# Moving the points of sums, products and score visits in a three-engine schedule of attention and a gated MLP

## Chip, cores, metric

The kernel runs on one core of one Trainium2 chip. The metric is the device time of one execution in microseconds (us). The traces record it at full or at half speed. Engines: PE is TensorE, DVE is VectorE, ACT is ScalarE, POOL is GpSimd, SP issues DMA transposes.

## The reference

Eight batches of gated attention with squared ReLU scores, then an MLP with g = h cos(h):

```python
B, S, D = u.shape                      # 8, 3008, 256; z has 64 columns
scores = np.matmul(z, z.transpose(0, 2, 1)) / S
attn = np.maximum(scores, 0.0) ** 2
x = (u * np.matmul(attn, v)).reshape(B * S, D)
h = x @ w_in                           # 256 -> 2048
out = (h * np.cos(h)) @ w_out          # 2048 -> 256
```

## The kernel before

Each batch has six column groups c of 512 tokens. The scores are symmetric, so a block (c, R) with R > c is computed once (a "score visit" computes up to three half blocks) and a DMA transpose makes its mirror (R, c).

```python
def s_squares(b, c, R, p, banks, on_act=False):      # cut
    ... nc.scalar.activation(rt[:, i, :], banks[i], AF.Relu)          # ACT
    ... nc.vector.tensor_tensor(sq, rv, rv, ALU.mult)                 # DVE (or ACT)
    if p == 1 and R > c ...: turn_s(b, c, R)                          # SP: DMA transpose
```

In 44 of the 48 groups (all but the first four of batch 0) attn @ v isn't multiplied out plainly over row blocks 0 to 4. As in Strassen's method, seven products replace eight: DVE first forms sums of quarters of the score blocks in place. `a_sums1` is the first, `a_sums2` the second, and products P1 to P7 read raw quarters (P1, P2, P4), first sums (P5, P6) and second sums (P3, P7):

```python
def a_sums1(b, c, team):                                 # cut
    s1 = quarters(b, c, team, (0, 1))                    # overwritten in place
    nc.vector.tensor_tensor(s1, s1, quarters(b, c, team, (1, 1)), ALU.add)         # L486
    nc.vector.tensor_tensor(s2(b, c, team[0], len(team)), s1,
                            quarters(b, c, team, (0, 0)), ALU.subtract)            # L488
def a_sums2(b, c, R):
    nc.vector.tensor_tensor(dst, src, sub, ALU.subtract)                           # L498
def keep(b, c, n):                                       # cut: combines the products
    if n in (1, 5): nc.scalar.copy(p15[:, n // 5, 0:h], acc[n // 5][:, h:2 * h])   # L544
    elif n == 6:    nc.vector.tensor_tensor(q[:, 0, 0:h], acc[0][:, h:2 * h],
                                            p15[:, 1, 0:h], ALU.add)               # L546
    elif n == 8:    ...   # RADD, L549        else: ...   # WADD, L555
def finish(b, c):                                        # cut: x = acc * u, frees acc
    nc.vector.tensor_tensor(x[:, nh, :], acc[nh][:, o:o + n], ut[:, nh, o:o + n], ALU.mult)  # L415
```

P1, P4, P6 and P7 go one after the other into the same columns of one PSUM bank (PSUM is the memory that PE's results go to), so the addition after P6 (L546) must have read them before P7 may write. Beside this run the MLP's matmuls (`h_quantum` L564 on PE, cos on ACT, g on DVE L571; `y_quantum` L581 on PE), which fill PE between the pieces.

Everything is put on a clock of 48 units per batch, 8 per group; the list of events is sorted by time, and that is the program order:

```python
at(t + SUM1[c][0] + 2 * SUM1[c][1] * i, 2, lambda: a_sums1(b, c, team))
at(t + SUM2[c][0] + SUM2[c][1] * i, 2.5, lambda: a_sums2(b, c, R))
at(t + o, 2, lambda: product(b, c, n))              # o from PLAN[c]; "A1"/"B1": a plain block
at(t + o + 0.02, 2.1, lambda: keep(b, c, n))        # after products 1, 5, 6, 7
at(t + 7.45, 2, lambda: finish(b, c))
t = b * span - lead + span * (i + VSHIFT.get(i, 0)) / len(visits)
scores.append((2 * math.floor(t / 2) + 1.2, some))  # score visit i
```

Of the kernel before, what the change touches and what calls it, by code (L numbers as in the profile page):

```python
# [14 lines left out]
def kernel(  # L15
# [32 lines left out]
    NSLOT = 18  # L48
    NW = 5
    PLAN = {  # L50
        0: [(0.75, 'P1 P2'), (1.0, 'P5'), (1.4, 'P6'), (2.75, 'P3'), (3.0, 'P7'),
            (5.0, 'P4'), (5.4, 'A1'), (6.15, 'A1'), (6.35, 'A1'), (6.55, 'B1'),
            (7.0, 'B2')],
        1: [(0.75, 'P1 P5 P2'), (2.15, 'P6'), (2.75, 'P7 P3'), (3.4, 'A2 B1'),
            (4.35, 'P4 B1'), (6.75, 'A1 B1')],
        2: [(0.75, 'P1 P5 P2'), (2.15, 'B1'), (2.35, 'P6'), (2.75, 'P7 B1'), (3.4, 'P3'),
            (4.15, 'P4'), (6.55, 'A1'), (6.75, 'A1'), (7.4, 'A1 B1')],
        3: [(0.75, 'P1 P2'), (1.0, 'P5'), (1.4, 'P6'), (2.75, 'P7'), (3.0, 'B1'),
            (3.4, 'P3'), (4.35, 'A1 B1'), (4.75, 'A1'), (5.4, 'B1'), (6.15, 'P4'),
            (6.75, 'A1')],  # L60
        4: [(0.75, 'P1 P2'), (1.0, 'P5'), (1.4, 'P6'), (4.15, 'P7'), (4.75, 'B1'),
            (5.4, 'P3 B1'), (6.35, 'P4 A1'), (7.0, 'A1'), (7.4, 'A1 B1')],
        5: [(0.75, 'P1 P2'), (1.4, 'P5'), (2.75, 'P6'), (3.0, 'P3'), (4.15, 'B1'),
            (4.55, 'P7'), (5.0, 'P4'), (5.4, 'B1'), (6.15, 'A1'), (6.55, 'A1'),
            (7.4, 'A1 B1')],
    }
    SUM1, SUM2, WADD, RADD = {0: (-3.5, 0.07), 1: (-2.25, 0.5), 2: (-1.85, 0.15), 3: (-2.85, 0.85), 4: (-3.05, 0.85), 5: (-2.3, 0.55)}, {0: (1.1, 0.02), 1: (0.8, 0.32), 2: (2.1, 0.02), 3: (1.45, 0.02), 4: (1.1, 0.17), 5: (1.55, 0.02)}, {0: 4.36, 1: 3.06, 2: 4.96, 3: 4.16, 4: 6.06, 5: 5.76}, {0: 2.05, 1: 3.35, 2: 3.55, 3: 5.25, 4: 4.25, 5: 0.95}
    TSUM = [-1.9, 0.5, -0.4]
    WSET = {0: [0, 1, 2, 3, 4], 1: [0, 1, 2, 3, 4], 2: [0, 1, 2, 3, 4], 3: [0, 1, 2, 3, 4], 4: [0, 1, 2, 3, 4], 5: [0, 1, 2, 3, 4]}
    VAT = [-13, -3.9, -4.5]  # L70
    HOFF, YOFF = [0.3, 0.3, 0.4, 0.6], [0.6, 0.6, 0.6, 0.7]
    HALF = {0: 3.3, 1: 4.75, 2: 6.9, 3: 6.0, 4: 9.2, 5: 4.7}

    inv_s = 1.0 / float(S)
    inv_s2 = inv_s * inv_s
# [156 lines left out]
    def direct(b, c, R):  # L232


        return b == 0 and c <= 2

    def triangle(b, c, R):

        return R == c and (b, c) > (0, NC // 2)
# [190 lines left out]
    def v_sums(b, g):  # L430

        n = min(2, NW - 2 * g)
        t = vs(b, g)[:, 0:n * K, :].rearrange("p (r k) (d w) -> p r k d w", r=n, w=P)
        o = vsum[:, 2 * g:2 * g + n]
        for d in range(2):
            ins = nc.vector.tensor_tensor(
                o[:, :, 2 * d], t[:, :, 2 * d:2 * d + 2, 1], t[:, :, 0:2, d], ALU.subtract).ins
            if d == 0:
                after(ins, before[-1], NOSYNC)
        nc.vector.tensor_tensor(o[:, :, 1], t[:, :, 2:4, 1], o[:, :, 0], ALU.subtract)  # L440
        nc.vector.tensor_tensor(o[:, :, 3], t[:, :, 2:4, 0], o[:, :, 1], ALU.subtract)
        for R in range(2 * g, 2 * g + n):
            summed[R] = b
# [156 lines left out]
    def at(t, rank, f):  # L600
        events.append((t, rank, len(events), f))
# [4 lines left out]
    groups = [(c, R) for c in range(NC) for R in range(c, NC)]  # L606
    span = NC * U
    lead = 2.0 * U
    VSHIFT = {4: 0.0, 13: 0.55, 1: 0.54, 5: 0.0, 2: 0.0, 12: 1.09, 10: 0.27, 7: 0.55, 0: 0.28, 6: 0.29, 9: -0.82, 3: -0.28, 11: 0.54, 8: 0.0}

    items = [(c, R, p) for c, R in groups for p in ((2,) if c == R else (0, 1))]
    for c, before_item in {5: (4, 5, 0)}.items():
# [8 lines left out]
    visits = []  # L621
# [10 lines left out]
    for b in range(B):  # L632
        for i, some in enumerate(visits):
            some = [(b, c, R, q) for c, R, p in some if not direct(b, c, R)
                    for q in ((0, 1) if p == 2 and not triangle(b, c, R) else (p,))]
            t = b * span - lead + span * (i + VSHIFT.get(i, 0)) / len(visits)
            if some:
                scores.append((2 * math.floor(t / 2) + 1.2, some))
        for c in range(NC):
            if direct(b, c, c):  # L640
                for i in range(NC):
                    R = (c + i) % NC
                    scores.append((c * U + 4 * i / 3 - 3.1, [(b, c, R, 0), (b, c, R, 1)]))
# [19 lines left out]
    for t, some in scores:  # L663
        for b, c, R, p in some:
            use(("a", b, c, R), t, t + 1)
            if p == 1 and R > c and TURNS.get((b, c, R), t) is not None:
                t = TURNS.get((b, c, R), t)
                use(("t", b, c, R), t + 0.8, t + 2.5)
                use(("a", b, c, R), t, t + 3)
    for b in range(B):  # L670
        for g in range((NW + 1) // 2):
            at(b * span + (TSUM[g] if b else 3 * U + 1 + 2.5 * g), 2, lambda b=b, g=g: v_sums(b, g))
        for c in range(NC):
            t = b * span + c * U
            W = seven(b, c)
            d = direct(b, c, c)
            ready = 1.5 + when[(b, c, NC - 1)]
            first, last = (0.6, 6.93) if d else (HALF[c] if W else 1.0, 7.3)
            room = [i for i, sc in enumerate(scores)
# [60 lines left out]
    for m in range(NT):  # L740
        b, i = divmod((m + 1) * TW - 1, S)
# [10 lines left out]
    for b in range(B):  # L752
        t = b * span
# [73 lines left out]
```

## Time and profile before

| | before |
|---|---|
| time, 3 runs | 1226.01 us median, 1224.46 to 1227.6 |
| profiled span | 1222.9 us |
| busy PE, DVE, ACT | 1199.4, 1060.5, 864.1 us |
| PE idle in the span | 23.5 us |
| DMA transposes of score blocks | 249 |

One more stretch of the order of time is needed later, a score visit (visit 9) of the kernel before; columns are start, us, engine, line, what, and the idle time before it:

```profile
330.12 0.84 PE L261 MATMUL w<-zT 64*128 64x512 f16 x4
331.19 0.39 PE L261 MATMUL w<-zT 64*128 64x512 f16 x2 [0.23 <-DVE g L571]
331.41 0.39 PE L365 MATMUL acc<-s,v 64*128 64x512 f16 x2
```

The visit begins at 330.12 and the next matmul (L564) at 331.73, so it took 1.61 us. Only 0.23 us of that is recorded as idle.

### The profile page before, as it was taken

The page shows a single profiled execution, that of the slowest core. Times are in us where ns is not written, and L with a number is a line of the kernel's source. Part 1 is how long each engine was busy: PE and PEld are TensorE (multiplying, and loading weights), DVE is VectorE, ACT ScalarE, POOL GpSimd, SP SyncE. Part 2 cuts the span into 40 slices and gives each one's busy share as a digit, 9 for nine tenths or more (in the row PEclk, how much of TensorE's full clock was granted, in tenths as well). Part 3 has the DMA queues.
Part 4 walks back from the last instruction along what each step waited for, and adds up shares of the span by engine and source line. Part 5 has one row for each costly group of instructions (what it writes and reads, how often), then busy time and mean ns, then how long its engine had stood idle before and what let it go on. Part 6 is the DMA issues. An engine that isn't in the chain of part 4 may idle for free.

```text
span 1222.9 us, 23870 instructions
## 1 busy us (share of the span) xinstructions
PE 1199.4 (98%) x8853; PEld 808.8 (66%) x8853; DVE 1060.5 (87%) x1977; ACT 864.1 (71%) x1783; POOL 145.9 (12%) x201
## 2 busy tenths in 40 slices
PE   8999999999999999999999999999999999999998
PEld 3356766667667666676666766676666676666776
DVE  7889988899889898898988989889898899888974
ACT  6768686686866868668686687766877668776645
POOL 3220101001010110101101010011100111000000
PEclk9999999999999999999999999999999999999999
DMA  9999857789578986769778698776996769764411
GB/s 149 180 162 156 126 99 111 124 146 119 105 110 122 150 111 119 101 119 150 113 121 106 110 156 113 124 107 99 166 112 123 98 102 169 119 111 85 73 35 44
DMA packets 484228, 145.07 MB, mean 119 GB/s; under 512 B 432400, under 2 KB 484112, under 8 KB 484112
## 3 DMA queue, kind: packets, MB, share of 16 engines
q1 hardware_dynamic: 356448, 88.73, 42.7%
q0 software_dynamic: 100400, 29.77, 26.8%
q10 hardware_dynamic: 27264, 25.06, 6.8%
q8 instruction: 69, 1.13, 0.4%
q14 instruction: 47, 0.39, 0.1%
HBM read 60.29 MB, written 24.64 MB: 69 GB/s over the span
## 4 chain that ended last, share of the span: by engine, by line
PE 85%; DMA 7%; ACT 3%; DVE 3%; issue 1%; POOL 0%; DVEq 0%; ACTq 0%; POOLq 0%
PE acc L530 26%; PE w L564 23%; PE w L581 23%; PE acc L388 6%; DMA s<-s 6%; PE w L261 6%; ACT rt L317 2%; DVE g L571 2%; PE acc L365 1%; DMA w_out<-in_moe_w_out_dram 1%; ACT s L321 1%; DVE x L415 1%; ACT c L568 0%; DVE s L323 0%; PE w L784 0%
## 5 line engine op out<-in xcount | busy, mean ns | idle before, releaser
L568 ACT ACTIVATE c<-w 128x512 f16<-128x512 f32 x752 | 413.2, 628 | 138.6 <-PE w L564 62.5
L571 DVE TENSOR_TENSOR g<-w,c 128x512 f16<-128x512 f32 x752 | 475.9, 681 | 36.0 <-ACT c L568 34.0
L564 PE MATMUL w<-x,w_in 128*128 128x512 f16 x1504 | 368.6, 379 | 1.0 <-ACT rt L317 1.0
L581 PE MATMUL w<-w_out,g 128*128 128x256 f16 x3008 | 358.5, 273 | 1.6 <-DMA w_out<-in_moe_w_out_dram 1.6
L581 PEld LDWEIGHTS <-g 128*128 128x128 f16 x3008 | 294.2, 98 | 76.0 <-issue 4.3
L317 ACT ACTIVATE rt<-w 128x512 f16<-128x512 f32 x489 | 251.5, 612 | 38.2 <-PE w L261 38.2
L564 PEld LDWEIGHTS <-w_in 128*128 128x128 f16 x1504 | 145.7, 98 | 158.5 <-issue 13.9
L530 PE MATMUL acc<-s,vsum 128*128 128x256 f16 (+1 forms) x1760 | 216.1, 270 | 1.8 <-DVE s L486 1.8
L530 PEld LDWEIGHTS <-vsum 128*128 128x128 f16 x1760 | 169.3, 98 | 37.5 <-issue 13.4
L323 DVE TENSOR_TENSOR s<-rt 128x1024 f16<-128x1024 f16 x196 | 132.3, 687 | 56.5 <-ACT rt L317 55.8
L530 PE MATMUL acc<-s,v 128*128 128x256 f16 (+1 forms) x1320 | 157.7, 270 | 9.2 <-DVE x L415 9.2
L118 POOL DMA_DIRECT2D ust<-in_u_dram x112 | 81.0, 730 | 616.3 <-PE acc L388 402.0
L530 PEld LDWEIGHTS <-v 128*128 128x128 f16 x1320 | 127.4, 98 | 27.1 <-issue 12.3
L588 ACT ACTIVATE ob<-w 128x256 f32<-128x256 f32 x188 | 76.1, 405 | 85.3 <-PE w L581 85.1
L498 DVE TENSOR_TENSOR s<-s,s 128x1024 f16<-128x1024 f16 (+1 forms) x220 | 136.1, 669 | 0.0
L388 PE MATMUL acc<-s,v 128*128 128x512 f16 x448 | 133.4, 382 | 0.4 <-DVE s L323 0.3
L261 PE MATMUL w<-zT 64*128 64x512 f16 (+3 forms) x684 | 93.8, 360 | 4.1 <-DVE g L571 1.9
L486 DVE TENSOR_TENSOR s<-s 128x1024 f16<-128x1024 f16 (+2 forms) x132 | 76.4, 583 | 19.9 <-DMA s<-s 19.5
L488 DVE TENSOR_TENSOR s<-s 128x1024 f16<-128x1024 f16 (+2 forms) x132 | 76.5, 584 | 1.1
L388 PEld LDWEIGHTS <-v 128*128 128x128 f16 x448 | 39.4, 98 | 50.3 <-issue 25.0
L544 ACT COPY p<-acc 128x256 f32<-128x256 f32 (+1 forms) x88 | 32.7, 372 | 55.4 <-PE acc L530 54.7
L415 DVE TENSOR_TENSOR x<-acc,ut 128x512 f16<-128x512 f32 (+7 forms) x112 | 64.3, 595 | 1.5 <-PE acc L388 1.5
(39 smaller groups left out, 440.6 us busy)
## 6 DMA issues: line engine op xcount, KB each, us to landing
out_dram<-ob ACTq DMA_DIRECT2D x92, 256.0 KB, 2.8
ust<-in_u_dram POOLq DMA_DIRECT2D x80, 128.0 KB, 5.0
v<-in_v_dram POOLq DMA_DIRECT2D x16, 512.0 KB, 7.6
s<-s SPq DMA_TRANSPOSE x249, 4.4
v<-in_v_dram POOLq DMA_DIRECT2D x8, 448.0 KB, 5.9
zst<-in_z_dram POOLq DMA_DIRECT2D x14, 128.0 KB, 4.9
ust<-in_u_dram POOLq DMA_DIRECT2D x16, 96.0 KB, 3.8
w_in<-in_moe_w_in_dram POOLq DMA_DIRECT2D x4, 256.0 KB, 5.8
```

The costliest lines, as they stand in the source:

```text
L118: hold(nc.gpsimd.dma_start(dst, src))
L261: chain(nc.tensor.matmul(out, zt[h, R * K + k + 1 - lo, :], zt[h, j0 + s0:j0 + K, :].rearrange("p j w -> p (j w)"), start=True, stop=True, ...
L317: nc.scalar.activation(rt[:, i, :], banks[i], AF.Relu)
L323: ins = nc.vector.tensor_tensor(sq, rv, rv, ALU.mult).ins
L388: chain(nc.tensor.matmul(acc[:, 0:wn], vs(b, j // G)[:, j % G, nh * P:(nh + 1) * P], a, start=(start and n == 0), stop=(last and n == len( ...
L415: ins = nc.vector.tensor_tensor(x[:, nh, :], acc[nh][:, o:o + n], ut[:, nh, o:o + n], ALU.mult).ins
L498: after(nc.vector.tensor_tensor(dst, src, sub, ALU.subtract).ins, before[-1], NOSYNC)
L530: chain(nc.tensor.matmul(acc[bank][:, cols], lhs[:, k, :], rhs[:, k, :] if old else rhs[:, :, k * P:(k + 1) * P], start=(n in (1, 5) and i ...
L564: chain(nc.tensor.matmul(hp, w_in16[:, k, ft * P:(ft + 1) * P], x[:, k, :], start=(k == 0), stop=(k == NDH - 1)))
L568: nc.scalar.activation(c16, hp, AF.Sin, bias=math.pi / 2.0, scale=inv_s2)
L571: nc.vector.tensor_tensor(gs[(m, ft // FG)][:, ft % FG, :], hp, c16, ALU.mult)
L581: chain(nc.tensor.matmul(ys[m][:, 0:D], gs[(m, f4)][:, ft % FG, ts * P:(ts + 1) * P], w_out16[:, ft, :], start=(ft == 0), stop=(ft == NFT ...
```

## The change

Its intent is to put the sums further behind the DMA transposes that still read the blocks they overwrite, and to move the products and visits to match. Work, operands and counts stay the same. VFIRST equals VSHIFT, so it does nothing by itself. The diff, unchanged context cut:

```diff
--- before.py
+++ after.py
@@ -48,28 +48,25 @@
-        0: [(0.75, 'P1 P2'), (1.0, 'P5'), (1.4, 'P6'), (2.75, 'P3'), (3.0, 'P7'),
-            (5.0, 'P4'), (5.4, 'A1'), (6.15, 'A1'), (6.35, 'A1'), (6.55, 'B1'),
-            (7.0, 'B2')],
-        1: [(0.75, 'P1 P5 P2'), (2.15, 'P6'), (2.75, 'P7 P3'), (3.4, 'A2 B1'),
-            (4.35, 'P4 B1'), (6.75, 'A1 B1')],
-        2: [(0.75, 'P1 P5 P2'), (2.15, 'B1'), (2.35, 'P6'), (2.75, 'P7 B1'), (3.4, 'P3'),
-            (4.15, 'P4'), (6.55, 'A1'), (6.75, 'A1'), (7.4, 'A1 B1')],
-        3: [(0.75, 'P1 P2'), (1.0, 'P5'), (1.4, 'P6'), (2.75, 'P7'), (3.0, 'B1'),
-            (3.4, 'P3'), (4.35, 'A1 B1'), (4.75, 'A1'), (5.4, 'B1'), (6.15, 'P4'),
-            (6.75, 'A1')],
-        4: [(0.75, 'P1 P2'), (1.0, 'P5'), (1.4, 'P6'), (4.15, 'P7'), (4.75, 'B1'),
-            (5.4, 'P3 B1'), (6.35, 'P4 A1'), (7.0, 'A1'), (7.4, 'A1 B1')],
-        5: [(0.75, 'P1 P2'), (1.4, 'P5'), (2.75, 'P6'), (3.0, 'P3'), (4.15, 'B1'),
-            (4.55, 'P7'), (5.0, 'P4'), (5.4, 'B1'), (6.15, 'A1'), (6.55, 'A1'),
-            (7.4, 'A1 B1')],
+        0: [(0.75, 'P1 P2'), (1.0, 'P5'), (1.4, 'P6'), (2.75, 'P7'), (4.15, 'P3'),
+            (5.0, 'P4'), (5.4, 'A2 B1'), (6.55, 'A1'), (6.75, 'B2')],
+        1: [(0.75, 'P1 P2'), (1.0, 'P5'), (2.15, 'P6'), (3.0, 'P7 P3'), (3.4, 'P4 A1'),
+            (6.15, 'A1'), (6.35, 'A1 B1'), (6.55, 'B1'), (7.4, 'B1')],
+        2: [(0.75, 'P1'), (1.0, 'P5 P2'), (1.4, 'P6'), (2.75, 'P7'), (3.0, 'P3 B1'),
+            (3.4, 'B1'), (4.15, 'P4'), (6.15, 'A1'), (6.35, 'B1'), (6.55, 'A2')],
+        3: [(1.0, 'P1 P2'), (1.4, 'P5'), (2.15, 'P6'), (2.75, 'P7'), (3.0, 'P3'),
+            (3.4, 'A1'), (4.15, 'P4 B2'), (5.0, 'A2 B1')],
+        4: [(0.75, 'P1 P2'), (1.0, 'P5'), (1.4, 'P6'), (2.75, 'P7'), (4.75, 'B1'),
+            (5.4, 'P3 B1'), (6.55, 'A1'), (6.75, 'P4 A1'), (7.4, 'A1 B1')],
+        5: [(0.75, 'P1 P2'), (1.4, 'P5'), (2.75, 'B1'), (3.0, 'P3'), (4.15, 'P6'),
+            (4.55, 'P7'), (5.0, 'P4'), (5.4, 'B1'), (6.15, 'A1'), (7.4, 'A2 B1')],
-    SUM1, SUM2, WADD, RADD = {0: (-3.5, 0.07), 1: (-2.25, 0.5), 2: (-1.85, 0.15), 3: (-2.85, 0.85), 4: (-3.05, 0.85), 5: (-2.3, 0.55)}, {0: (1.1, 0.02), 1: (0.8, 0.32), 2: (2.1, 0.02), 3: (1.45, 0.02), 4: (1.1, 0.17), 5: (1.55, 0.02)}, {0: 4.36, 1: 3.06, 2: 4.96, 3: 4.16, 4: 6.06, 5: 5.76}, {0: 2.05, 1: 3.35, 2: 3.55, 3: 5.25, 4: 4.25, 5: 0.95}
-    TSUM = [-1.9, 0.5, -0.4]
+    SUM1, SUM2, WADD, RADD = {0: (-3.5, 0.07), 1: (-2.5, 0.7), 2: (-0.6, 0.15), 3: (-1.85, 0.6), 4: (-2.55, 0.85), 5: (-2.3, 0.55)}, {0: (1.1, 0.12), 1: (1.05, 0.22), 2: (2.1, 0.02), 3: (1.45, 0.12), 4: (1.1, 0.22), 5: (1.55, 0.02)}, {0: 4.86, 1: 3.56, 2: 4.36, 3: 3.56, 4: 6.76, 5: 6.26}, {0: 4.05, 1: 4.35, 2: 2.85, 3: 5.25, 4: 5.15, 5: 2.95}
+    TSUM = [-1.4, 0.5, -1.9]
-    HOFF, YOFF = [0.3, 0.3, 0.4, 0.6], [0.6, 0.6, 0.6, 0.7]
-    HALF = {0: 3.3, 1: 4.75, 2: 6.9, 3: 6.0, 4: 9.2, 5: 4.7}
+    HOFF, YOFF = [0.3, 0.3, 0.3, 0.6], [0.6, 0.6, 0.6, 0.7]
+    HALF = {0: 4.8, 1: 3.15, 2: 4.0, 3: 8.4, 4: 9.2, 5: 4.7}
@@ -606,7 +603,8 @@
-    VSHIFT = {4: 0.0, 13: 0.55, 1: 0.54, 5: 0.0, 2: 0.0, 12: 1.09, 10: 0.27, 7: 0.55, 0: 0.28, 6: 0.29, 9: -0.82, 3: -0.28, 11: 0.54, 8: 0.0}
+    VSHIFT = {4: -0.01, 13: 0.82, 1: 0.82, 5: -0.27, 2: -0.29, 12: 0.54, 10: 0.0, 7: 1.09, 0: 0.28, 6: 0.02, 9: -0.28, 3: -0.28, 11: -0.01, 8: -0.82}
+    VFIRST = VSHIFT
@@ -633,7 +631,7 @@
-            t = b * span - lead + span * (i + VSHIFT.get(i, 0)) / len(visits)
+            t = b * span - lead + span * (i + (VSHIFT if b else VFIRST).get(i, 0)) / len(visits)
```

## The prediction

> **What bounds the kernel now.** I read the busy shares first, then the waits of TensorE (PE), then the order of time around the largest of them, then the windows by batch. The page's first part:
>
> ```profile
> PE 1199.4 (98%) x8853; PEld 808.8 (66%) x8853; DVE 1060.5 (87%) x1977; ACT 864.1 (71%) x1783; POOL 145.9 (12%) x201
> ```
>
> PE is the bound, and it is idle for only 1222.9 - 1199.4 = 23.5 us of the whole span. Busy is not yet "at its peak", so I checked the pace: in the order of time a stretch of eight 512-column matmuls takes 1.90 us (shown below), and with 0.38 us for the last one that is (1.90 - 0.38)/7 = 0.217 us from start to start. Nothing in the change alters the number, shape or operands of a matmul. So what the change can win lies in PE's gaps. The view of waits of PE, first for the span after 80 us, then two of its lines for the whole span:
>
> ```profile
> PE acc L530 <- DVE x L415: 9.2, 7, 2.0
> PE w L261 <- DVE g L571: 1.9, 8, 0.3
> PE acc L530 <- DVE s L486: 1.8, 3, 0.9
> ...
> PE w L581 <- DMA w_out<-in_moe_w_out_dram: 1.6, 1, 1.6
> PE w L261 <- ACT zT L224: 1.6, 2, 1.1
> ```
>
> (us in total, times, longest.) After the first 80 us three kinds of wait are left, 9.2 + 1.9 + 1.8 = 12.9 us. Everything else is the start (first turns of z, w_out) and the tail, which the change doesn't touch. The seven waits of 9.2 us come once per batch, 152 us apart. One of them, in order of time (start, us, engine, line, what, and in brackets the idle time before it):
>
> ```profile
> 331.73 1.90 PE L564 MATMUL w<-x,w_in 128*128 128x512 f16 x8
> ...
> 337.37 1.91 PE L581 MATMUL w<-w_out,g 128*128 128x256 f16 x16
> ...
> 339.61 0.69 DVE L486 TENSOR_TENSOR s<-s 128x1024 f16<-128x1024 f16 x1 [2.19 <-DMA s<-s]
> 340.22 0.68 DVE L415 TENSOR_TENSOR x<-acc,ut 128x512 f16<-128x512 f32 x1
> 340.82 0.68 DVE L488 TENSOR_TENSOR s<-s 128x1024 f16<-128x1024 f16 x1
> 340.96 1.25 PE L530 MATMUL acc<-s,v 128*128 128x256 f16 x10 [1.67 <-DVE x L415]
> ```
>
> The reader is to see a chain. A sum of group 2 (L486) overwrites in place a block of squared scores that a DMA transpose still reads. It waits 2.19 us for it. Behind it in VectorE's (DVE's) queue stands L415, the multiplication by u that empties group 1's accumulator, and PE's first product of group 2 (L530) needs that accumulator. So the DMA is charged to PE although the product itself didn't need it. Group 3 has the milder form: its last sum waits for a DMA and product 5 reads that sum directly (the 1.8 us). VectorE's view of waits gives the source in one line:
>
> ```profile
> DVE s L486 <- DMA s<-s: 19.5, 14, 2.6
> ```
>
> Fourteen waits, 19.5 us, of which PE feels 9.2 + 1.8 = 11.0; the rest falls in VectorE's slack. A window of one batch, 188:340 us, shows how much slack:
>
> ```profile
> 188.00:340.00 152.00, 149.79 (x1128) 103.40 (x1128) 134.45 (x253) 109.89 (x229) 17.87 (x24) 1.00 0.78 121
> ```
>
> (PE, weight load, DVE, ACT, POOL busy, clock, DMA share, GB/s.) VectorE has 152 - 134.45 = 17.6 us free per batch, 12%, so shifting its order is possible, but not by much at one place.
>
> **What the Trainium skill says.** "Perfetto Trace Analysis", the section Per-instruction lifecycle, says that ACT and DVE take their instructions strictly first in, first out, and that waiting for semaphores lies outside the recorded window. The fence above agrees: L415's inputs were complete (group 1's last matmuls end by 335.8), it still started at 340.22, behind the blocked L486, and the block shows as an idle gap of 2.19 us. The same section says that a DMA's recorded issue doesn't hold the data movement. Agreed too: here the transpose in question was issued at 332.43, its record is 2 us long, but it landed at 339.52, 7.1 us later. The view of tile s gives 2.3/4.4/12.5 us from issue to landing for all transposes (shortest, median, longest). "DMA: Bandwidth & Descriptors", section Issuing engines are not separate DMA queues, says that transfers of all issuers interleave on the same engines; this fits 7.1 us where the median is 4.4, as two loads of u were issued at 332.10, though no run here isolates it.
>
> **The change part by part.** Nothing is added or removed; VFIRST equals VSHIFT. The program's clock has 48 units per batch, so a unit is 152/48 = 3.17 us. For each group I worked out from the numbers in the diff how far a sum stands behind the score visit that starts the transpose it depends on (units, before -> after): group 1's last pair 2.55 -> 3.1; group 2's last pair 1.55 -> 2.8; group 3's last block 1.35 -> 3.35; group 4's last block 3.15 -> 5.65; groups 0 and 5 stay at 3.6 and more. The two shortest, 1.55 (4.9 us) and 1.35 (4.3 us), are those where the waits are. From the visit's place to landing is some 9 us in the case above (visit on PE at about 330, landed 339.52), and the new distances are 2.8 x 3.17 = 8.9 us and 10.6 us, to which VectorE's own lag behind PE of 1.5 to 2 us is added. So both waits for the DMA should go.
>
> Group 2, step by step. The sums move from -1.85 to -0.6 with 0.3 per team: now 15.4, 15.7, 16.0, with the emptying of group 1 at 15.45. So only the first team (1.37 us: L486 and L488 at 0.68 each) stands in front of L415, and it has no young transpose. L415 then ends in time or nearly so: VectorE's g products end near 337.3 (they hang on ACT), plus 1.37, plus 0.68 for the first half makes 339.3, where PE arrives at 339.2. That removes 9.2 us. But product 5 now follows the sums closely. PE from the point 16.0 (335.6) to product 5's fourth block: eight h matmuls 1.73, sixteen y matmuls 1.75, product 1 1.09 and three blocks 0.65 = 5.2 us, so 340.9. VectorE: 337.3 + 1.37 + L415 1.36 + second team 0.83 + L486 0.68 = 341.5. A new wait of about 0.6 us, which may be 0 if the scheduler sends L486s ahead, so I take 0.4 x 7 batches = 2.8 us. Net gain 6.4 us.
>
> Group 3: its visit 11 comes 2 units earlier, the sum stays at 24.55. Gain 1.8 us. Its second team now stands right before the emptying of group 2 (23.35 against 23.45): 1.37 + 1.3 us on VectorE in the 3.5 us that PE spends on h and y before product 1. No wait expected.
>
> Visits 7 and 8 trade places, so the two-pair visit instead of the three-pair one stands before visit 9, where PE waits 0.24 us in each batch for a PSUM buffer (the 1.9 us). I take half: 1.0 us.
>
> The many moved P, A and B points (PLAN) mostly fall in stretches with no other PE event between old and new place (24.75 to 25.0, 34.75 to 36.15), so PE's order hardly changes; L365's half blocks stay next to a visit, so no more switches between 64 and 128 rows. I count 0. Sum: 6.4 + 1.8 + 1.0 = 9.2 us, 1226.0 - 9.2 = 1216.8 us.
>
> **The rivals.** (1) The wait only moves: L486 now holds up product 5 of group 2 instead of L415 holding up product 1. Against it, 1.25 units more distance for the DMA; for it, the 0.6 us of working above. If the DMA is still late the full 1.3 us a batch comes back, and the time is 1223. (2) VectorE or ACT becomes the bound where visits bunch: 10 and 11 now follow each other at 19.2 and 21.2. For it, VectorE's 88% in the batch; against it, visits 12, 13 and 0 are spread out (27.2, 31.2, 33.2 instead of 29.2, 31.2, 33.2), and today three visits in a row cost only 0.24 us. It would add 0.3 to 0.6 us a batch, 1219 to 1221. (3) All waits go, and with them the slower restart after each: 1226 - 12.9 - 1.6 = 1211.5, the 1.6 being about 0.16 us of slower first matmuls after some ten long waits.
>
> **Range and chances.** Rival 3 gives the lower end, 1211, rival 1 the upper, 1223. Faster by over 2% means below 1201.5, 24.5 us less, more than the 23.5 us that PE is idle in all, start and tail included: practically excluded. Slower by over 2% would need new waits of 3 us in every batch, against the purpose of each shift. So faster 0.01, same 0.97, slower 0.02.
>
> **What would show it right or wrong.** Right: in the changed kernel's waits of PE, L415 falls from 9.2 to under 2 us, VectorE's wait for DMA s<-s from 19.5 to under 6, PE busy stays near 1199 and the span falls with the idle time. Wait of L530 for L486 up to 3 us would show the price at product 5; more would be rival 1. A longer wait of L261 for L571 or L317 would be rival 2. I am wrong if PE busy itself changes by over 3 us, since then the order of matmuls costs something that I counted as zero, or if L530 waits for L498, the second sums.

## The result

| | before | after |
|---|---|---|
| median, range | 1225.49 us (1224.46 to 1227.6), 4 runs | 1207.45 us (1206.15 to 1209.4), 4 runs |
| profiled span | 1222.9 us | 1204.0 us |
| PE busy / idle | 1199.4 / 23.5 us | 1193.9 / 10.1 us |

The ratio is 0.9852, 95% interval 0.9833 to 0.9871. Ratios here are the mean time of one kernel's fast runs over the mean of the other's fast runs of the same rounds, so they differ slightly from the ratio of the medians quoted. By the 2% rule the class is "same", but the gain of 18 us is clear of noise, and the time lies below my range of 1211 to 1223.

The busy line of the page after, and then PE's waits after 80 us:

```profile
PE 1193.9 (99%) x8853; PEld 809.7 (67%) x8853; DVE 1056.1 (88%) x1977; ACT 859.6 (71%) x1783; POOL 145.9 (12%) x201
```

```profile
PE w L258 <- DMA zT<-zst: 2.0, 1, 2.0
PE acc L527 <- DVE vsum L433: 0.5, 3, 0.2
```

All three waits of before (12.9 us) are gone from this view; one of 2.0 us and three small ones (0.5 us in all) are new. In the whole view of waits after there is no line any more of DVE waiting for DMA s<-s, where 19.5 us stood. (After the change the lines are numbered 3 lower from the products on: L412 is the multiplication by u, L483 and L485 are the first sums, L495 the second, L543 the addition after product 6, L568 g.) But PE's busy time fell too, by 5.5 us, with the same 8853 matmuls. That is the first sign that idle time isn't all that was lost.

The place of the old wait, group 2 of the same batch, in order of time after the change:

```profile
329.58 0.68 DVE L412 TENSOR_TENSOR x<-acc,ut 128x512 f16<-128x512 f32 x1
...
333.67 0.68 DVE L483 TENSOR_TENSOR s<-s 128x1024 f16<-128x1024 f16 x1
...
334.26 0.69 DVE L412 TENSOR_TENSOR x<-acc,ut 128x512 f16<-128x512 f32 x1
334.87 0.68 DVE L485 TENSOR_TENSOR s<-s 128x1024 f16<-128x1024 f16 x1
335.46 1.02 DVE L483 TENSOR_TENSOR s<-s 128x512 f16<-128x512 f16 x2
335.55 1.25 PE L527 MATMUL acc<-s,v 128*128 128x256 f16 x10
...
336.64 1.26 PE L527 MATMUL acc<-s,vsum 128*128 128x256 f16 x10
...
339.74 0.68 DVE L495 TENSOR_TENSOR s<-s,s 128x1024 f16<-128x1024 f16 x1
...
340.33 0.42 DVE L543 TENSOR_TENSOR q<-acc,p 128x256 f32<-128x256 f32 x1
340.67 1.89 DVE L495 TENSOR_TENSOR s<-s,s 128x1024 f16<-128x1024 f16 x3
```

Product 1 starts at 335.55 with no wait before it, product 5 at 336.64 likewise: the last first sums (the x2 line) were done by 336.48. The first half of L412 ran at 329.58, long before, since the new PLAN ends bank 0 of group 1 earlier. And L543, the addition after product 6, stands between the second sums (L495), not behind all five.

And visit 9 after the change:

```profile
326.45 0.91 PE L258 MATMUL w<-zT 64*128 64x512 f16 x6
...
327.13 0.44 PE L362 MATMUL acc<-s,v 64*128 64x512 f16 x2
327.51 0.39 PE L385 MATMUL acc<-s,v 128*128 128x512 f16 x1
```

From 326.45 to 327.51 the same eight matmuls took 1.06 us, 0.55 us less than before, where the view showed only 0.23 us of idle time to win. A 512-column matmul is drawn 0.38 us long though the next one starts 0.217 us later when nothing waits. A wait shorter than the difference, 0.16 us, hides wholly inside the drawn end of the matmul before it, and of each longer wait 0.16 us is hidden.

To count this I added up the start-to-start times of all PE instructions over six steady batches (from visit 12 of one batch to visit 12 of the next) and compared them with the full pace of each kind in the same traces: 216 ns for 512 columns, 109 for 256, 96 for 224, 95 ns more where the next matmul uses 64 rows instead of 128, and for a visit the shortest burst of its kind (969 ns for eight with half blocks, 753 for six). "Idle" is what the profile records as gaps, "hidden" the rest. The clock doesn't explain the rest: it is recorded at full speed through these batches of both traces. Nor need all of it be waiting: 0.51 us stay in the run e9_core below, which has no idle time.

| us per batch | total | full pace | idle | hidden |
|---|---|---|---|---|
| before | 151.65 | 148.18 | 1.86 | 1.61 |
| after | 149.12 | 148.18 | 0.13 | 0.81 |

The full pace is the same to 0.01 us, so the order of matmuls costs nothing by itself. Of the 2.53 us won per batch 1.73 are idle and 0.80 hidden: 0.44 in score visits, 0.21 in front of the products' matmuls (L530), where each of the old waits had hidden its 0.16, and 0.16 behind h matmuls (L564). Of these some six a batch were followed 59 ns late before and none after, but one or two waits of about 0.2 us a batch at other h matmuls took half of that back.

### The profile page after: what moved, and what is told of

Same layout as the page of the kernel before. It is cut to its first block, busy times and chain, and to the rows that moved or that the text cites. A ratio compares the mean times of both kernels' runs of the same rounds, so it can differ in the third digit from the quotient of the medians.

```text
span 1204.0 us, 23873 instructions
## 1 busy us (share of the span) xinstructions
PE 1193.9 (99%) x8853; PEld 809.7 (67%) x8853; DVE 1056.1 (88%) x1977; ACT 859.6 (71%) x1783; POOL 145.9 (12%) x201
## 4 chain that ended last, share of the span: by engine, by line
PE 88%; DVE 5%; DMA 3%; ACT 2%; issue 2%; POOL 0%; SPq 0%; ACTq 0%; DVEq 0%; POOLq 0%
PE acc L527 26%; PE w L578 25%; PE w L561 24%; PE acc L385 6%; PE w L258 6%; DMA v<-in_v_dram 2%; DVE g L568 2%; ACT rt L314 1%; DVE x L412 1%; PE acc L362 1%; DMA w_out<-in_moe_w_out_dram 1%; DVE s L320 1%; DVE s L485 0%; DVE s L483 0%; DMA zT<-zst 0%
## 5 line engine op out<-in xcount | busy, mean ns | idle before, releaser
L568 DVE TENSOR_TENSOR g<-w,c 128x512 f16<-128x512 f32 x752 | 472.1, 683 | 22.3 <-ACT c L565 18.2
L561 PE MATMUL w<-x,w_in 128*128 128x512 f16 x1504 | 363.5, 379 | 1.4 <-ACT rt L314 1.0
L561 PEld LDWEIGHTS <-w_in 128*128 128x128 f16 x1504 | 146.5, 98 | 157.5 <-issue 7.9
L527 PEld LDWEIGHTS <-v 128*128 128x128 f16 x1320 | 128.1, 98 | 15.5 <-issue 2.1
L495 DVE TENSOR_TENSOR s<-s,s 128x1024 f16<-128x1024 f16 (+1 forms) x220 | 138.0, 672 | 0.1
L385 PE MATMUL acc<-s,v 128*128 128x512 f16 x448 | 128.1, 381 | 0.1
L258 PE MATMUL w<-zT 64*128 64x512 f16 (+3 forms) x684 | 91.4, 362 | 3.6 <-DMA zT<-zst 2.0
L485 DVE TENSOR_TENSOR s<-s 128x1024 f16<-128x1024 f16 (+2 forms) x132 | 76.2, 586 | 0.8
L483 DVE TENSOR_TENSOR s<-s 128x1024 f16<-128x1024 f16 (+2 forms) x132 | 75.9, 584 | 0.0
L541 ACT COPY p<-acc 128x256 f32<-128x256 f32 (+1 forms) x88 | 32.7, 372 | 60.4 <-PE acc L527 60.2
L412 DVE TENSOR_TENSOR x<-acc,ut 128x512 f16<-128x512 f32 (+7 forms) x112 | 65.7, 598 | 2.6 <-PE acc L385 2.6
```

What stands on the lines that cost most here:

```text
L258: chain(nc.tensor.matmul(out, zt[h, R * K + k + 1 - lo, :], zt[h, j0 + s0:j0 + K, :].rearrange("p j w -> p (j w)"), start=True, stop=True, ...
L385: chain(nc.tensor.matmul(acc[:, 0:wn], vs(b, j // G)[:, j % G, nh * P:(nh + 1) * P], a, start=(start and n == 0), stop=(last and n == len( ...
L412: ins = nc.vector.tensor_tensor(x[:, nh, :], acc[nh][:, o:o + n], ut[:, nh, o:o + n], ALU.mult).ins
L495: after(nc.vector.tensor_tensor(dst, src, sub, ALU.subtract).ins, before[-1], NOSYNC)
L527: chain(nc.tensor.matmul(acc[bank][:, cols], lhs[:, k, :], rhs[:, k, :] if old else rhs[:, :, k * P:(k + 1) * P], start=(n in (1, 5) and i ...
L561: chain(nc.tensor.matmul(hp, w_in16[:, k, ft * P:(ft + 1) * P], x[:, k, :], start=(k == 0), stop=(k == NDH - 1)))
```

## The experiments

Below, S is the new SUM1, V the new VSHIFT, P the new PLAN. All kernels gave the reference's result except where said. Each ratio is to the kernel before in the same rounds; that kernel itself ran between 1221.2 and 1233.5 us, so for a few us I rely on the waits and on the sums by batch. Part of this scatter is the clock: the kernel before took 1222.1 us at a mean of 1.0 and 1233.5 at 0.993. One wait outside the batches differs from run to run with no edit that bears on it: PE's for w_out near 73 us, 0.2 us in after, 1.6 in before, 2.5 when after ran again, up to 4.4 in the others. Where it took 2.5 to 4.4 us, a half-speed stretch of the clock stands beside it in five profiles (e4, e9, e13, e18, e19), in two it doesn't (e6, e16).

### One large part alone

**S alone**, with PE's order of instructions the same as before:

```diff
-SUM1 = {..., 1: (-2.25, 0.5), 2: (-1.85, 0.15), 3: (-2.85, 0.85), 4: (-3.05, 0.85), ...}
+SUM1 = {..., 1: (-2.5, 0.7),  2: (-0.6, 0.15),  3: (-1.85, 0.6),  4: (-2.55, 0.85), ...}
```

> The kernel before with the new SUM1 points alone (first sums); PE's order of instructions is the same as before. Theory A (the sum that waits for a DMA stands in front of the multiplication by u in VectorE's queue, and the new point of group 2 alone cures that): PE's wait of L530 for L415 falls from 9.2 to under 1 us, no wait at product 5, gain 10 to 12 us, some 1214 us. Rival as predicted (the wait partly comes back at product 5): L530 waits for L486 about 3 us, gain 6 to 7 us. Rival B (the gain of L415 came from PLAN, which ends bank 0 of group 1 earlier): L415's wait stays over 5 us, gain under 5 us. Group 3's wait for L486 (1.8 us) should stay or shrink only a little, as its last sum stays at 24.55 behind visit 11 at 23.2. Stalls inside score visits stay as before.

Measured 1224.78 us, ratio 0.9989 (0.9955 to 1.0024): no gain. PE's waits in this run:

```profile
PE acc L530 <- DVE q L546: 9.3, 7, 1.4
PE acc L530 <- DVE s L486: 1.8, 3, 0.8
...
PE w L261 <- DVE g L571: 1.6, 7, 0.2
```

The 9.2 us for L415 are gone, as theory A said, and so are 14 of DVE's 19.5 us of waiting for the DMA (5.4 left). Product 5 doesn't wait for L486, against my prediction. But 9.3 us for L546 have taken the place. The order of time shows why:

```profile
341.98 1.25 PE L530 MATMUL acc<-s,vsum 128*128 128x256 f16 x10
342.51 3.09 DVE L498 TENSOR_TENSOR s<-s,s 128x1024 f16<-128x1024 f16 x5
...
345.52 1.28 DVE L571 TENSOR_TENSOR g<-w,c 128x512 f16<-128x512 f32 x2
...
346.72 0.42 DVE L546 TENSOR_TENSOR q<-acc,p 128x256 f32<-128x256 f32 x1
...
347.19 1.25 PE L530 MATMUL acc<-s,vsum 128*128 128x256 f16 x10 [1.34 <-DVE q L546]
```

Product 6 ends at 343.2, yet the addition that reads it (L546, point 2.37 of the group) stands in DVE's queue behind five second sums (points from 2.1) and two g, and product 7 waits for it. The sums that were blocked before now run undelayed, but later, and push DVE's other work back at the next place where PE needs it.

**V alone**:

```diff
-VSHIFT = {4: 0.0, 13: 0.55, ..., 12: 1.09, 7: 0.55, 9: -0.82, 8: 0.0, ...}
+VSHIFT = {4: -0.01, 13: 0.82, ..., 12: 0.54, 7: 1.09, 9: -0.28, 8: -0.82, ...}
```

> The kernel before with the new VSHIFT alone (score visits). Theory A: visit 9 with the two-pair visit in front runs near its floor of 969 ns instead of 1607, of which the idle time shows only 0.23 us, so about 0.6 us a batch is won there, and group 3's wait for its young transpose (L530 for L486, 1.8 us) goes; L415's wait stays near 9 us because visit 9 itself and group 2's sums don't move. Gain 5 to 7 us in all, some 1219 us; PE busy time falls by 3 us or more although no matmul changed. Rival: hidden stalls have nothing to do with the visits; gain under 3 us and PE busy as before.

Measured 1232.46 us, ratio 1.0046 (1.0013 to 1.0079): slower. In the trace visit 9's excess over full pace fell from 0.64 to 0.10 us a batch, as expected, and group 3's wait for L486 is gone. L415's wait, which I expected to stay near 9 us, fell to 1.8, and DVE's waiting for the DMA from 19.5 to 11.2, so the visits' places bear on this wait too (how, I did not follow up). But the steady batches lost 0.89 us each, 0.20 of it full pace (as in e9_core below), and these waits came instead:

```profile
PE w L564 <- DVE g L571: 5.0, 13, 1.1
PE acc L530 <- DVE acc L549: 4.1, 7, 0.6
```

**P alone**, at first with the old SUM2:

> The kernel before with the new PLAN alone (products and plain blocks). Theory A: nearly no PE event lies between most old and new places, the sums still wait for the DMA in front of L415: time within 3 us of before, L415's wait over 6 us. Rival B (in group 1 the blocks of bank 0 now end at 6.35 and those of bank 1 at 7.4, so bank 0 is emptied well before the blocked sum and product 1 of group 2, which writes bank 0, starts in time): L415's wait under 3 us, gain of 6 us or more.

This one was wrong (relative error 0.24) and 1251.46 us. The mistake is in the cut: the old SUM2 puts the first second sum of group 1 at 0.8, the new PLAN puts product 5, which must read the quarter before it is overwritten, at 1.0. The run says nothing of the theories, only that PLAN and SUM2 can't be parted. Done right:

```diff
 # the kernel before with PLAN and SUM2 of after
-1: [(0.75, 'P1 P5 P2'), (2.15, 'P6'), ...        SUM2 1: (0.8, 0.32)
+1: [(0.75, 'P1 P2'), (1.0, 'P5'), (2.15, 'P6'), ...  SUM2 1: (1.05, 0.22)
```

> e3_plan done right: new PLAN together with SUM2, which it needs (with the old one the second sum of group 1 overwrote a quarter before product 5 read it, hence its wrong result). Theory C: the sums still stand in front of L415 behind the DMA, PE's wait for L415 stays over 6 us, time within 4 us of before. Rival B (bank 0 emptied earlier by the new order of plain blocks shields product 1): L415's wait under 3 us, gain of 6 us or more.

Measured 1232.03 us, ratio 1.0045 (1.0002 to 1.0088). L415's wait fell to 0.7 us although the DMA still held DVE for 19.8 us: rival B was right about the mechanism, bank 0 is emptied early enough. Its gain didn't come: 4.5 us of waits for ScalarE's copy L541, more waits at the visits (L258 for g 3.7 us, L561 for L281 2.5 us) and 1.50 us a batch hidden in score visits stand in its place.

So each of the three parts alone gives nothing or costs some 5 us.

### One large part undone

> The kernel after with the old SUM1 points alone. Theory A: the sum of group 2 at 14.75 again stands 1.55 units behind visit 9, VectorE waits for DMA s<-s over 8 us in all, and if that alone decides, L527's wait for L412 is back to 7 us or more and the time rises by 8 to 11 us. Rival B (PLAN's early end of bank 0 shields product 1): VectorE waits for the DMA again, but PE doesn't feel it; time within 3 us of after.

The kernel after with the old SUM1: 1231.51 us, ratio to before 1.0049 (1.0016 to 1.0083), so 24 us of median above after. Both theories missed it: L412's wait didn't return (the early bank 0 shields it), but the DMA blocks DVE again, for 19.4 us, and behind the blocked sum now stand g products:

```profile
PE w L561 <- DVE g L568: 16.1, 15, 2.0
```

In order of time, one of the seven places:

```profile
493.03 0.43 DVE L483 TENSOR_TENSOR s<-s 128x512 f16<-128x512 f16 x1 [2.16 <-DMA s<-s]
493.38 0.68 DVE L568 TENSOR_TENSOR g<-w,c 128x512 f16<-128x512 f32 x1
...
494.11 0.59 PE L561 MATMUL w<-x,w_in 128*128 128x512 f16 x2 [1.06 <-DVE g L568]
...
495.64 1.06 PE L561 MATMUL w<-x,w_in 128*128 128x512 f16 x4 [0.94 <-DVE g L568]
...
496.50 3.58 PE L578 MATMUL w<-w_out,g 128*128 128x256 f16 x16
```

PE stops for PSUM buffers that g would free. The waits aren't all: the 16 y matmuls of the last line are drawn 3.58 us long where 1.91 is usual, and from 496.50 on the clock is recorded at half speed for 3.41 us. Such a stretch stands in five of the seven batches beside a pair of these waits of 1.9 to 3.0 us together; two pairs, of 2.2 and 2.3 us, have none, and what halves the clock was not tested. Against after, a steady batch loses 3.81 us, 2.26 idle and 1.55 hidden, of this 0.99 at y matmuls. All four runs of e4 had a mean clock of 0.992 or 0.993. With the new products a late sum costs more than it did with the old ones.

> The kernel after with the old VSHIFT. Theory C with the hidden stalls (the visits are worth some 0.6 us per batch inside visit 9 and the group 3 wait of 1.8 us in all): 6 to 9 us slower than after, that is 1213 to 1217, with the first burst of eight 64-row matmuls near 1.6 us again. Rival (everything is tuned to everything, each part undone breaks the rest): over 15 us slower than after, as undoing the sums was (24 us).

The kernel after with the old VSHIFT: 1229.37 us, ratio to before 1.0034 (0.9978 to 1.009), 22 us above after. The rival was right. The trace shows the loss in three visits: beyond full pace visit 9 lost 1.31 us a batch, visit 12 0.42 and visit 13 1.00, together 2.73, where after loses 0.09. The sums and products alone, with the old visits, give the same picture:

> The kernel before with new SUM1, SUM2 and PLAN, old visits and small offsets. Theory C: at least the gain of e5_sums_p6, 10 to 13 us; the stalls inside score visits (0.68 us per batch hidden, 0.29 idle) and the waits for L486 in group 3 stay, since the visits are old. Rival D: waits reappear elsewhere, gain under 5 us.

Before with S, P and SUM2: 1228.68 us, ratio 1.0017 (0.9971 to 1.0062). L415's wait is gone, and hidden time rose from 1.61 to 2.57 us a batch, 1.71 of it in visits. The small rest of the change (WADD, RADD, TSUM, HOFF, HALF) makes no difference between this run and the one before it.

### The core of group 2, step by step

Since e1 named the reader that was left behind, I moved only that one. S plus product 6 of group 2:

```diff
-2: [(0.75, 'P1 P5 P2'), (2.15, 'B1'), (2.35, 'P6'), (2.75, 'P7 B1'), ...
+2: [(0.75, 'P1 P5 P2'), (1.4, 'P6'), (2.15, 'B1'), (2.75, 'P7 B1'), ...
```

> The kernel before with the new SUM1 points and one product moved: product 6 of group 2 from 2.35 to 1.4. In e1_sums the wait of 9.2 us (L415) was gone, but 9.3 us of wait for L546 had come in its place: the addition after product 6 stood in VectorE's queue behind the five second sums (3.1 us) of group 2, because its point 2.37 lies behind theirs at 2.1. Theory C (the first sums' points and product 6's point are a pair, and this pair is the core of the gain): L546's wait falls under 1 us, L415's stays gone, gain 10 to 12 us against before. Rival D (VectorE is simply late at this place because the sums now fall into its busy stretch; moving one product moves the wait to the next reader of VectorE's results, L498 or L549 or L571): PE's idle time after 80 us stays over 8 us, gain under 4 us.

Measured 1219.9 us, ratio 0.9948 (0.9904 to 0.9992), less than expected (0.59 us per steady batch, some 4 us over seven). L546's wait went, as theory C said, and half of it came back one step on:

```profile
PE acc L530 <- ACT p L544: 4.7, 7, 0.7
```

Product 6 waits for the copy of product 1 by ScalarE (L544), whose event at 0.77 follows products 1, 5 and 2, all at 0.75. In the trace the group's two copies start at 339.58, when product 5 had ended, and at 340.89, when product 2 had ended too; product 6 starts at 341.31, when the second is done. The new PLAN of group 2 has 'P1' at 0.75 and 'P5 P2' at 1.0, which puts the copy in between. So, S plus the new PLAN of group 2 alone:

```diff
-2: [(0.75, 'P1 P5 P2'), (2.15, 'B1'), (2.35, 'P6'), (2.75, 'P7 B1'), (3.4, 'P3'), ...
+2: [(0.75, 'P1'), (1.0, 'P5 P2'), (1.4, 'P6'), (2.75, 'P7'), (3.0, 'P3 B1'), ...
```

> The kernel before with the new SUM1 and the new PLAN of group 2 alone. In e5_sums_p6 product 6 waited 4.7 us for ScalarE's copy of product 1 (L544), which began only when products 5 and 2, emitted before it, had ended as well. The new PLAN of group 2 puts product 1 at 0.75 and products 5 and 2 at 1.0, so that the copy at 0.77 stands between them. Theory C: the waits for L544, L546 and L415 are all under 1 us now, and only the visits' stalls and group 3's 1.8 us stay: per batch idle about 0.45 us, hidden about 1.7 us, gain 10 to 13 us against before (1212 to 1216). Rival D: yet another reader of VectorE waits in its place and the gain stays at the 5 us of e5_sums_p6 or less.

Measured 1215.91 us, ratio 0.9929 (0.9903 to 0.9955), some 9 us faster than before; the median is at the upper edge of what was expected. After 80 us this is left of PE's waits:

```profile
PE acc L530 <- DVE s L486: 2.1, 3, 1.2
...
PE w L261 <- DVE g L571: 1.6, 7, 0.2
```

Per batch the idle time fell from 1.86 to 0.52 us; the hidden time stayed (1.68). The undoing in the kernel after, PLAN of group 2 old and all else new:

> The kernel after with the old PLAN of group 2 alone, the undoing of the same step. Theory C: waits for L543 (addition after product 6) or L541 (copy of product 1) come back with about 1.3 us in each of 7 batches, 8 to 12 us slower than after, some 1217. Rival D: the place is not special; under 4 us slower.

Measured 1217.51 us, ratio to before 0.9936 (0.9913 to 0.996), 10 us of median above after, and the same wait is back:

```profile
PE acc L527 <- DVE q L543: 7.7, 7, 1.1
```

Theory C holds both ways: the first sums and the order of group 2's products 1, 5, 2 and 6 around DVE's additions are one unit, worth about 9 to 10 us. Two limits: the runs moved the first sums of four groups at once, so that group 2's alone do it is read from the traces, and its other products and plain blocks moved along with these four.

### The rest

> The kernel before with new SUM1, SUM2, PLAN, WADD, RADD and VSHIFT; old stay only TSUM (sums of v), HOFF and HALF. Expected of theory C: the three large parts make up nearly all of the gain, within 3 us of after (1207 to 1211). Rival: the package needs every number, over 6 us slower than after.

S, SUM2, P, WADD, RADD and V on the kernel before: 1205.3 us, ratio 0.9837 (0.9817 to 0.9857), all of the gain. In its steady batches PE has no recorded idle time at all (148.89 us a batch, hidden 0.51). Its full pace is 148.38 instead of 148.18, because with the old HALF one pair of half blocks per batch stands apart from a visit and pays its own switch of rows.

> e13_sums_plan2 (1215.9) with the new VSHIFT added. If the visits only need the pair: visit 9's stall of 0.64 us a batch and group 3's 2.1 us of wait go, 5 to 7 us faster than e13, some 1210. If they need the moved additions or the other products too: the waits for L549 (4.1 us in e2_visits) and L571 at L564 (5.0 us) stay, within 3 us of e13 or slower.

V added to e13: 1221.89 us, ratio 0.9952 (0.9911 to 0.9993). It got worse, so the visits don't merely need the pair. L486's wait of group 3 is gone, but 4.1 us for L549 and 2.12 us of hidden time a batch are there.

> e16_pair_visits with the new SUM2, WADD and RADD as well, so that of the large parts only PLAN of the other five groups is old. If the additions were what the visits lacked: L549's wait is gone and the time is 3 us or more below e16, near 1208. If PLAN of the other groups is needed: the waits for L571 remain and the time stays within 2 us of e16.

With SUM2, WADD and RADD as well: 1223.6 us, ratio 0.9969 (0.9932 to 1.0005). L549's 4.1 us stay, and 3.3 us for the other addition (L555) come on top. So the additions weren't what was missing. Since e9_core differs from this kernel only in PLAN of the other five groups, the visits need those: they are what turns V from a loss into a gain. Which of the five groups matters most I did not separate.

### A faster version

In the kernel after visit 0 of batch 1 waited 2.0 us for zT, whose second transpose was issued behind those of visit 12. One edit puts it ahead:

```diff
-at(t - 2.5 * U, 0, lambda b=b: turn_z(b))
+at(t - 2.65 * U, 0, lambda b=b: turn_z(b))
```

> The kernel after with the DMA transposes of z for the next batch at 26.8 instead of 28.0, ahead of visit 12 at 27.2 in the DMA queue's order. In after, visit 0 of batch 1 waits 2.0 us for the second of them, which was issued at 86.6 behind four of visit 12's transposes (issues at 76.4 to 80.3) and three more. Expected: that single wait goes, 1.5 to 2.5 us faster than after; later batches as they are. Rival: the triangle transposes now come later and group 4's last sum waits for the DMA in every batch; 1 to 5 us slower than after.

Measured 1204.79 us, ratio to before 0.9841 (0.9822 to 0.9859). The wait for zT is gone; by the intervals the time isn't told apart from that of after (0.9852).

> The kernel after with the old TSUM and HOFF: e9_core plus the new HALF. In e9_core PE's steady batches had no idle time at all and took 148.89 us, of them 148.38 at full pace; after has a floor of 148.18, as its half blocks of v (L362) all lie beside a visit, while with the old HALF and new visits some pay their own switch between 64 and 128 rows, 0.2 us a batch. Expected: floor 148.18 and no idle, 148.7 us a batch, 1.4 us faster than e9_core and 2 to 3 faster than after, some 1203 to 1204. Rival: HALF moves half blocks into the way of visits and hidden stalls come back; 1206 or more.

The kernel after with the old TSUM and HOFF: 1205.77 us, ratio 0.9817 (0.9783 to 0.9851), not told apart from after by its interval; per batch 148.97 us, less gain than expected. Both edits together, beside the kernel after on the same chip:

> The kernel after with the transposes of z at 26.8 (as e7_early_z) and the old TSUM and HOFF (as e15_best). The 2.0 to 2.3 us of wait for zT go, 0.1 to 0.2 us a batch of small stalls go: 2 to 4 us faster than e19_after_again. If the gains are below what rounds resolve: within 1.5 us of it.

> The kernel after, unchanged, as the yardstick for e18 on this chip. Expected 1206 to 1209, ratio to before 0.983 to 0.987.

1203.06 us (1202.42 to 1205.36, 6 runs; ratio 0.9821, 0.9798 to 0.9843) against 1208.63 us (1208.43 to 1210.12, 6 runs; ratio 0.9863, 0.9839 to 0.9888). The ranges don't overlap, so this version beats both kernels, by 0.4% against after. How the 5.6 us divide isn't settled: when after ran again its profile had no wait for zT but one of 2.5 us for w_out before it, so a delay at w_out can hide the one for zT; the batches differ by 0.19 us (148.81 against 149.00), some 1.3 us over seven; and the clock granted was 0.997 to 0.999 in the repeat of after and 0.999 to 1.0 in the other. The clock isn't all: at the same 0.999, two runs of the new version took 1205.3 and 1205.4 us, four of after 1208.4 to 1210.1. But of the 3.6 us between the two profiled runs 1.4 arose before 15.5 us, where after's clock was at half speed for 3.41 us and neither edit had begun to act.

## Why the prediction was wrong

- **The bound and the chain.** Right: PE is the bound, a sum that waits for a DMA blocked L415 in DVE's queue. e1 moved the sums alone and exactly this wait disappeared. One reading there was loose: the 7.1 us from issue to landing of a whole block belong beside 5.4, the median of the 117 transposes of whole blocks, not beside 4.4, that of all 249.
- **The price at product 5, 0.4 us a batch, 2.8 us in all.** Wrong, it measured 0 in e1 and in after. DVE needed 2.73 us from the end of g (333.75) to the end of the last L483 (336.48), where I had added up 4.2: instructions followed each other every 0.60 us and not 0.68, the scheduler sent the L483s ahead of their L485s, and one half of L412 had run earlier. So the L415 term was 9.2 us and not 6.4 net, plus its slow restarts.
- **"The many moved P, A and B points (PLAN) mostly fall in stretches with no other PE event ... I count 0."** This is the step that failed. I looked at what a moved point does to PE's order and not at what it does to DVE's and ACT's. P6 of group 2 from 2.35 to 1.4 changes which side of five second sums its addition stands on, and P1 apart from P5 and P2 lets ACT's copy start earlier. Without both, the sums gave no gain clear of noise (e1), with them 9 (e13). I had named the rival "the wait only moves" but put it at product 5; it moved to product 7.
- **The ceiling of 12.9 + 1.6 = 14.5 us.** Wrong, and with it the lower end of the range. It took idle time for all that could be won. Hidden time of up to 1.61 us a batch, 11 us over seven batches, was missing but for the 1.6; 0.80 us a batch of it was won. This is the larger part of the miss in the number: 5.5 of the 9.7 us between the 9.2 predicted and the 18.9 of the profiles. I had the number for it in hand (0.38 us drawn against 0.217 us of pace) and used it only to say that the pace was good. The sign I named for being wrong, PE busy changing by over 3 us, came true at 5.5 us, but for this reason and not for the order of matmuls.
- **Visits, 1.0 us.** The direction was right in the end, the size wrong: visit 9's excess fell from 0.64 to 0.09 us a batch, 3.8 us over seven batches. But it isn't a term that can be added: V alone costs 0.5% (e2), and with the new products its absence costs 22 us (e8).
- **Group 3, 1.8 us.** Right in kind. The wait is gone after, it stays without V (e13: 2.1 us) and goes with it (e16).
- **"The start ... which the change doesn't touch."** Not quite: a new wait for zT of 2.0 us came, and w_out's fell from 1.6 to 0.2, though the latter varies without any edit.

In one sum over profiled spans: 18.9 us, of which 13.4 recorded as idle and 5.5 as busy, against 9.2 predicted, all of it idle. Of the 13.4, 10.1 lie between 80 us and the last matmul, 2.3 before and 1.0 after. The part before 80 us is not clearly the change's: PE's idle time there was 6.4 us in before, 4.1 in after and 7.4 when after ran again.

Left open: which of the five other groups' plans the new visits depend on, how e18's 5.6 us divide between the transposes, the offsets and the clock, and what halves the clock in e4.

## What to carry to other kernels

Take PE's headroom from start-to-start times against full pace, not from its gaps: with matmuls drawn longer than their spacing, every short wait hides in "busy". When you move an instruction on a queue that is served in order, list what stands behind it on each engine before and after, and move the readers that would be left behind (here a sum, an addition and a copy) in the same step. In a schedule where three engines are 71 to 99% busy, don't judge a part of a change by itself: three parts that each cost nothing or 0.5% gave 1.5% together.

## What the Trainium skill lacked or had wrong

- "Perfetto Trace Analysis", Per-instruction lifecycle, says that the end of a TensorE instruction is estimated, but not how much waiting this hides: with 0.38 us drawn and 0.217 us of pace up to 0.16 us per wait, at most 1.61 us of 151.65 per batch here, where 1.86 show as idle. What it says of DVE and ACT being strictly first in, first out agrees with the runs: moving one sum off the front of L415 removed 9.2 us of wait.
- "TensorE: Matmul & The Clock Gate", Back-to-back issue gap, gives two figures for 512 columns, some 216 ns isolated and 131 ns sustained in a stream of weight loads and matmuls. Here such a stream ran at 216 ns for 512 columns and 109 for 256 at 128 rows; the shortest step behind a 512-column matmul of 128 rows was 214 ns in six batches of before, and none came near 131.
- "TensorEngine Tiling (Array Packing)", Key Properties, says that changing the tiling mode drains the engine, without a number. Here the step from 128 to 64 rows cost 95 ns (311 ns from start to start behind a 512-column matmul, 205 behind one of 256).
- "DMA: Bandwidth & Descriptors", Latency and other measured facts, gives of the time of DMA transposes only a rate. What this schedule hangs on is the time to landing, 4.2 us at the shortest, 5.4 at the median and 12.5 at the longest for the 117 transposes of whole score blocks before the change, among loads on the same engines.
